# Block-sparse attention with a cosine MLP: tile 2 transposed by DMA, twenty small instructions moved from VectorE to GpSimd, and a new order of the program

## The chip, the cores and the metric

The kernel runs on one core of one Trainium2 chip. The time is that of one execution on the device, in microseconds; a comparison takes the median of several executions. TensorE is called PE below, VectorE DVE, ScalarE ACT, GpSimd POOL, and the queue from which most transfers are issued SP.

## What is computed

An attention over 4 batches of 8 heads, 768 positions and 64 columns, in which most blocks of 32 queries see only their neighbours, the first and last block, and three sampled blocks; then, on its 3072 x 512 result, an MLP whose activation is h cos(h). q, k and v are f32; the two weight matrices lie in DRAM as 64-bit floats.

```python
scores = scale * np.matmul(q, k.transpose(0, 1, 3, 2))
mask = np.abs(blk_i - blk_j) <= window
mask = mask | (blk_i == 0) | (blk_j == 0) | (blk_i == n_blocks - 1) | (blk_j == n_blocks - 1)
for qb in range(n_blocks):
    for kb in sampled_blocks[qb]:
        mask[qb * block:(qb + 1) * block, kb * block:(kb + 1) * block] = True
scores = np.where(mask, scores, -1000000000.0)
scores = scores - np.max(scores, axis=-1, keepdims=True)
attn = np.exp(scores)
attn = attn / (np.sum(attn, axis=-1, keepdims=True) + 1e-09)
...
h = x @ w_in
g = h * np.cos(h)
return (g @ w_out).astype(np.float32)
```

## The kernel before

**Tiles.** The attention runs over 24 tiles of 128 queries, numbered 0 to 23, six to a batch: five sparse ones and one dense (tile 5 is the first dense one). A sparse tile has four units, each with two heads; a dense one has eight. The MLP has 12 steps of two tiles each, and each step computes four column groups up (`m`, L1722) and down again (`d`, L1772). Operands that need more than f16 holds go as a high and a low half, so a matrix product is three products.

**A unit of a sparse tile.** PE makes the scores (L1377, L1386). DVE adds the mask to them and takes the row maxima (`add_max`, L1417), two instructions a unit. One DVE instruction on 128x2 elements (`neg_max`, L1432, operation `nb`) turns the maxima into the bias of the exponentials. ACT takes two exponentials with it (L1438). Then the probabilities must be split in halves and transposed for PE, which is done in one of two ways:

- By PE: three 128x128 f32 transpositions for each head (`p_turn`, operation `PF`, which issues through `turn32` at L1667 or L1669), then the high half by ACT from PSUM (`turned_hi`, L1459) and the low half by DVE (`turned_lo`, L1463; in tiles 0 and 1 by PE and ACT instead). The list `PF` has a 1 for each unit of tiles 0 to 4 that goes so; in the kernel before these are all units of tiles 0, 1 and 2.
- By DMA: ACT writes the high half into a buffer of a ring of three (`p_hi`, L1448), DVE the low half (`p_lo`, L1452), and SP issues one transposing DMA from the ring into one of the three PT buffers (`p_transpose`, L1473, operation `PT`).

Then PE multiplies by the values (`pv`, L1483 for the gathered blocks and L1500 for the rest; L1516 in a dense tile). Each tile's result is normalized (L1539), split (L1541, L1543), and transposed into the MLP's input `xT`, by PE in the tiles whose entry in the list `XF` is 1, by a DMA on SP otherwise (`x_transpose`, L1562).

**Other work beside it.** In the first 180 us the weights are loaded by SP in 32 pieces (`w_load`, L1592, operation `wl`; piece 17's is `wl17`), converted from 64 to 32 bits by DVE (`f64_to_f32`, L1600 to L1604, operation `wc`), scaled and split. A piece lands in a raw buffer, which must have been read by the conversions of an earlier piece before the next load into it is issued: pieces 16 and 17 land where pieces 12 and 13 were. POOL issues the gathers of V blocks (`v_gather`, L1330), four to a sparse tile, and copies K blocks (L1252); these wait for V's buffers, of which there are two.

**The order.** Nothing is ordered at run time but by semaphores: each engine runs its own list in order. These lists are made when the program is built: a planner (`Plan.op` and `Plan.run`) takes each operation with its engine, its predecessors and a place, and issues them by place. The table PLACES gives the place of every operation by its name: `mx2_0_1`, for instance, is `add_max` of tile 2, unit 0, second half. SP runs its transfers in this order as well, and one that has to wait for its source or its destination holds up those behind it.

The bias is made so:

```python
def neg_max(self, n, qc, mx, nb):
    nc, nu = self.nc, qc[:, 5:6]
    if self.seq[n][1] == self.NS:
        nc.vector.tensor_tensor(mx[:, 0:2], mx[:, 0:2], mx[:, 2:4], ALU.max)
    nc.vector.tensor_scalar(nb, mx[:, 0:2], nu, LN_PSCALE, op0=ALU.mult, op1=ALU.add)
```

Of the kernel before, what the change touches and what calls it, by code (L numbers as in the profile page):

```python
# [17 lines left out]
ALU = mybir.AluOpType  # L18
# [7 lines left out]
LN_PSCALE = 14.0 * math.log(2.0)  # L26
# [19 lines left out]
    PF=[1, 1, 1, 1, 1, 1, 1, 1, 1, 1, 1, 1, 0, 0, 0, 0, 0, 0, 0, 0], PC=["ph", "ph"], XF=[1, 1, 1, 0, 0, 0], XC="ph", UF=[1, 1, 1, 1, 0, 0], UC="ph", KF=[1] * 6, KC=["ph"] * 6,  # L46
# [5 lines left out]
    WGP=[0, 1, 1, 1, 1], WCP=[0] * 16, WCE=[0] * 16,  # L52
# [9 lines left out]
idx 0 sx 1 regs2_1 2 regs1_1 3 const_ident 4 ql1 5 qsq1 6 regs0_1 7 kload0_0 8 ksq0_0 9 kload0_1 10 const_pool 11 const_a 12 const_gidx 13 regs1_0 14  # L62
qsp1 15 kload0_2 16 const_samples 17 regs0_0 18 ksq0_1 19 ksq0_2 20 kred0 21 kall0s 22 qsc1c 23 ql0 24 qsc1e 25 regs3_1 26 vload0_0 27 const_b1 28
qsc1s 29 kall0 30 vload0_1 31 qsq0 32 qsp0 33 qsc0c 34 ksc0c 35 qsc0e 36 vload0_2 37 ksc0e 38 qhi1 39 qu0 40 ksc0s 41 vsq0_0 42 qnu0 43 khi0_1_0 44
khi0_1_1 45 qlo1 46 khi0_0_2 47 qsc0s 48 qhi0 49 vsq0_1 50 qu1 51 vsq0_2 52 wl1 53 ql2 54 klo0_1_0 55 klo0_1_1 56 khi0_0_1 57 klo0_0_2 58 wl2 59 qlo0
60 khi0_0_0 61 vred0 62 vall0s 63 klo0_0_1 64 vall0 65 khi0_1_2 66 qsq2 67 vsc0c 68 wc1_0 69 vsc0e 70 regs1_3 71 klo0_1_2 72 vsc0s 73 klo0_0_0 74
vhi0_5 75 ql3 76 vhi0_0 77 qk0_1 78 vhi0_4 79 wl0 80 qk0_0 81 wc1_1 82 vlo0_5 83 const_b 84 const_w 85 vlo0_0 86 vst0_0 87 vlo0_4 88 vhi0_2 89 wgd0 90
qsp2 91 qsc2c 92 wga0 93 qo0_0 94 qk0_2 95 qk0_3 96 qo0_3 97 qo0_2 98 vhi0_1 99 vst0_4 100 vlo0_2 101 vhi0_3 102 vst0_5 103 vlo0_1 104 qsq3 105 qo0_1
106 vst0_2 107 const_c 108 qsc2e 109 mx0_0_0 110 regs4_1 111 wc0_0 112 qsc2s 113 vst0_1 114 vlo0_3 115 mx0_0_1 116 qk1_1 117 const_n 118 mx0_1_0 119
nb0_0 120 wc0_1 121 vst0_3 122 mx0_1_1 123 ex0_0_0 124 wc0_2 125 mx0_2_0 126 ex0_0_1 127 mx0_3_0 128 qsp3 129 mx0_3_1 130 PF0_0_0 131 PF0_0_1 132 qnu1  # L70
133 qhi2 134 wl3 135 nb0_1 136 ex0_1_0 137 ph0_0_0 138 nb0_3 139 ph0_0_1 140 mx0_2_1 141 regs1_2 142 ex0_1_1 143 nb0_2 144 qu2 145 ex0_2_0 146 qk1_0
147 PG0_0_0 148 PG0_0_1 149 wgd1 150 pg0_0_1 151 qlo2 152 ex0_2_1 153 wc1_2 154 wga1 155 qo1_0 156 qo1_1 157 mx1_0_0 158 mx1_0_1 159 qsc3c 160 wl4 161
PF0_1_0 162 wc3_0 163 qsc3e 164 qu3 165 vg0_0 166 PF0_2_1 167 ex0_3_0 168 nb1_0 169 vg1_0 170 ph0_1_0 171 qsc3s 172 PF0_2_0 173 ph0_2_0 174 vg0_2 175
PF0_1_1 176 ph0_1_1 177 PG0_1_0 178 wsq0 179 pg0_1_0 180 wc3_1 181 vi0_0 182 pg0_0_0 183 ex1_0_0 184 vi0_1 185 ph0_2_1 186 mx1_1_0 187 wsq1 188
ex1_0_1 189 qk1_3 190 wl5 191 PG0_2_0 192 PG0_1_1 193 mx1_1_1 194 vg1_1 195 wc3_2 196 wsq3 197 qk1_2 198 pg0_2_0 199 regs2_3 200 vg0_1 201 ex0_3_1 202
PG0_2_1 203 regs3_0 204 wred0 205 wall0s 206 wall0 207 wsc0c 208 pg0_1_1 209 pg0_2_1 210 qnu2 211 nb1_1 212 qo1_3 213 qnu3 214 wc5_0 215 qo1_2 216 ql4
217 qsq4 218 mx1_3_0 219 ex1_1_1 220 qhi3 221 PF0_3_0 222 vi0_3 223 ex1_1_0 224 wc5_1 225 vi0_2 226 wsc0e 227 pv0_0 228 mx1_3_1 229 wsc0s 230 rs0 231
PF0_3_1 232 PF1_0_1 233 po0_0 234 wl7 235 po0_1 236 po0_2 237 ph0_3_0 238 ph0_3_1 239 PG0_3_1 240 whi2 241 wc5_2 242 nb1_3 243 pg0_3_1 244 regs2_0 245
PG0_3_0 246 wl6 247 qsp4 248 pg0_3_0 249 mx1_2_0 250 vi1_1 251 vg1_2 252 rr0 253 pv0_1 254 PF1_0_0 255 wl8 256 wgd2 257 wc7_0 258 whi0 259 ex1_3_0 260
wl9 261 ph1_0_0 262 mx1_2_1 263 pv0_2 264 PF1_1_0 265 wc7_1 266 wga2 267 pv0_3 268 ph1_0_1 269 qk2_0 270 qo2_0 271 mx2_0_0 272 ex1_3_1 273 qsc4c 274  # L80
mx2_0_1 275 PG1_0_0 276 PF1_1_1 277 PG1_0_1 278 vi1_2 279 wsi0 280 qlo3 281 wc7_2 282 ql5 283 qsc4e 284 ph1_1_0 285 pg1_0_0 286 PG1_1_0 287 wlm1 288
nb1_2 289 ph1_1_1 290 pg1_0_1 291 wsq5 292 pg1_1_0 293 nb2_0 294 wl11 295 qk2_1 296 qu4 297 qo2_1 298 PG1_1_1 299 wsq7 300 pg1_1_1 301 vi1_0 302 wlm0
303 pv1_0 304 ex1_2_1 305 mx2_1_0 306 mx2_1_1 307 wred4 308 wc9_0 309 ex1_2_0 310 regs4_3 311 wl10 312 wall4s 313 wlp1 314 po0_3 315 wlp0 316 wall4
317 PF1_3_0 318 ph1_3_0 319 wsc4c 320 PF1_3_1 321 wc9_1 322 wsc4e 323 wlm3 324 pv1_1 325 PF1_2_0 326 ex2_0_0 327 no0 328 PF1_2_1 329 vi1_3 330 qk2_3
331 ph1_3_1 332 regs4_0 333 sce0 334 PG1_3_0 335 vg2_0 336 rs1 337 qo2_3 338 po1_0 339 ex2_0_1 340 wc9_2 341 pg1_3_0 342 mx2_3_0 343 qsq5 344 ph1_2_0
345 PG1_3_1 346 mx2_3_1 347 vi2_2 348 wlp3 349 qsc4s 350 wsc4s 351 rr1 352 ph1_2_1 353 wlm2 354 pg1_3_1 355 wc11_0 356 vi2_1 357 wsi4 358 PG1_2_0 359
PF2_0_0 360 regs3_3 361 nb2_3 362 pg1_2_0 363 wc11_1 364 nb2_1 365 qk2_2 366 whi4 367 qsp5 368 qsc5c 369 qo2_2 370 wl13 371 po1_3 372 po1_1 373 wlp2
374 PG1_2_1 375 PF2_0_1 376 pg1_2_1 377 wlm5 378 wl12 379 wgd3 380 wc11_2 381 qhi4 382 vg2_2 383 wsq9 384 mx2_2_0 385 XF0 386 wl15 387 qsc5e 388 pv1_2
389 mx2_2_1 390 wga3 391 vg2_1 392 ph2_0_0 393 pl2_0_0 394 turn0_0 395 ex2_1_0 396 wlm4 397 qk3_0 398 qo3_0 399 ph2_0_1 400 pl2_0_1 401 nb2_2 402 qu5
403 pv1_3 404 wc13_0 405 mx3_0_0 406 qlo4 407 po1_2 408 wlp5 409 no1 410 xh0 411 whi6 412 ex2_3_1 413 ex2_2_0 414 wsq11 415 ex2_2_1 416 wlm7 417  # L90
ex2_3_0 418 wl14 419 vg3_0 420 wc13_1 421 wred8 422 wc13_2 423 XG0 424 PF2_2_0 425 XF1 426 ph2_2_0 427 wall8s 428 wlm6 429 wall8 430 pl2_2_0 431
ex2_1_1 432 mx3_0_1 433 vi2_3 434 wsc8c 435 PF2_3_1 436 wc15_0 437 PF2_1_0 438 xh1 439 PF2_3_0 440 wsc8e 441 xg0 442 wlp6 443 wc14_0 444 wsq13 445
vi3_2 446 qnu5 447 wlp7 448 qk3_3 449 wc15_1 450 wc14_1 451 qo3_3 452 wlp4 453 ph2_3_0 454 mx3_3_0 455 mx3_3_1 456 ql6 457 nb3_0 458 wc15_2 459
PF2_2_1 460 ph2_3_1 461 wl16 462 rs2 463 wl17 464 pv2_0 465 XG1 466 pl2_3_0 467 qk3_1 468 xg1 469 PF2_1_1 470 ph2_2_1 471 qo3_1 472 qsq6 473 wc14_2
474 wl19 475 ex3_0_0 476 ex3_0_1 477 pl2_3_1 478 nb3_3 479 ex3_3_1 480 vi2_0 481 po2_0 482 wsq15 483 qk3_2 484 pl2_2_1 485 qo3_2 486 ex3_3_0 487 ph3_0
488 mx3_1_0 489 ph2_1_0 490 m0_0_0 491 mx3_1_1 492 mx3_2_0 493 wc17_0 494 qnu4 495 po2_3 496 wsc8s 497 wc17_1 498 m0_0_1 499 vg3_1 500 m0_0_2 501 wgd4
502 ph3_3 503 wc17_2 504 mx3_2_1 505 pv2_2 506 wred12 507 qsc5s 508 wga4 509 pl2_1_0 510 pl3_0 511 wall12s 512 m0_0_3 513 wl18 514 wl25 515 nb3_1 516
whi8 517 wc18_0 518 whi10 519 ph2_1_1 520 vi3_1 521 wl20 522 wc19_0 523 pl2_1_1 524 wsi8 525 ev0_0_0 526 wlm8 527 pv2_1 528 wlm11 529 ev0_0_1 530
wsq17 531 po2_1 532 ka0_0 533 nb3_2 534 pv2_3 535 wall12 536 qk4_0 537 wc18_1 538 qhi5 539 ex3_1_1 540 ex3_2_0 541 rr2 542 wsc12c 543 ex3_2_1 544
ph3_2 545 pl3_3 546 wlp11 547 kb0_0 548 qk4_3 549 wc19_1 550 wc18_2 551 wc19_2 552 pl3_2 553 qo4_0 554 wl21 555 wlm10 556 PT3_0 557 qo4_3 558 wsq18  # L100
559 wsc12e 560 wlp8 561 mx4_0_0 562 mx4_0_1 563 qk4_1 564 vi3_0 565 wsq19 566 mx4_3_0 567 mx4_3_1 568 vg3_2 569 sin0_0 570 nb4_0 571 wred16 572 qo4_1
573 nb4_3 574 PT3_3 575 qk4_2 576 mx4_1_0 577 mx4_1_1 578 wall16s 579 ex3_1_0 580 rs3 581 gm0_0 582 ex4_0_0 583 wlm9 584 po2_2 585 wall16 586 nb4_1
587 wsc12s 588 ph3_1 589 pl3_1 590 rr3 591 wsc16c 592 turn0_1 593 pv3_0 594 wlp10 595 wsc16e 596 qo4_2 597 mx4_2_0 598 wl22 599 wlp9 600 no2 601
ex4_0_1 602 wl23 603 m0_1_0 604 wsi12 605 m0_1_1 606 whi14 607 wsc16s 608 ex4_1_0 609 vi3_3 610 mx4_2_1 611 pv3_3 612 XF2 613 wc21_0 614 nb4_2 615
wc21_1 616 ex4_1_1 617 PT3_1 618 po3_0 619 po3_3 620 qlo5 621 m0_1_2 622 m0_1_3 623 wc21_2 624 gh0_0 625 gl0_0 626 vg5_0 627 ev0_1_0 628 regs4_2 629
# [314 lines left out]
def plan_kernel(env, B, H, S, D, DM, DFF, pr):  # L420

    pl = Plan()
    e = env
    NB = S // BLK
# [17 lines left out]
    def nudge(key, row, col, width):  # L442
        x = row * width + col
        return pr[key][x] if 0 <= x < len(pr[key]) else 0.0
# [1424 lines left out]
```

## Time and profile before

| what | value |
|---|---|
| median of 3 runs | 765.25 us (763.42 to 768.58) |
| the profiled execution's own time | 764.32 us |
| its span from the first to the last instruction | 762.5 us |
| mean granted clock of PE | 0.975 |
| PE busy | 710.7 us, 93% of the span |
| ACT busy | 633.2 us, 83% |
| DVE busy | 612.2 us, 80% |
| POOL busy | 126.4 us, 17% |

So 1.8 us of the execution's time lie around the span. The busy times are sums over the whole span; the stretches differ much, and the rows further down show them by stretch, with the busy time of each engine in it, the granted clock of PE as a share of full speed, and the mean share of the 16 DMA engines that is in use. A line's "idle before" is the time in which its engine stood still just ahead of it, with what ended most of that.

### The profile page before, as it was taken

How to read it: one execution, taken by the hardware profiler on the slowest of the kernel's cores; microseconds unless marked ns; L12 is line 12 of the kernel's file. 1: busy time of each engine (PE TensorE's matmuls, PEld its weight loads, DVE VectorE, ACT ScalarE, POOL GpSimd, SP SyncE). 2: the span in 40 equal slices, each digit the busy share in tenths (PEclk: the TensorE clock that was granted, in tenths of full speed). 3: DMA queues.
4: the chain of work that ended last, by engine and by line, in shares of the span. 5: the costliest groups of instructions: out<-in, count | busy, mean ns of one | idle time of the engine just before them, and what ended most of it. 6: DMA issues, size and time to landing. Idle time of an engine off the chain costs nothing.

```text
span 762.5 us, 24855 instructions
## 1 busy us (share of the span) xinstructions
PE 710.7 (93%) x10286; PEld 484.8 (64%) x10286; DVE 612.2 (80%) x1551; ACT 633.2 (83%) x1210; POOL 126.4 (17%) x164
## 2 busy tenths in 40 slices
PE   3679897999999999999989998999999999999997
PEld 2446563668576568467666676677677677676763
DVE  5979999999999788988968787799878877665361
ACT  4689899999799888999987897998988987866342
POOL 6744402000401201020210302010311020000000
PEclk9589999999999999999999999999999999999999
DMA  7876889688838999999965799897949895446101
GB/s 281 242 234 216 265 198 249 157 216 189 211 90 149 180 191 181 229 208 220 196 112 108 171 185 203 165 206 140 192 79 172 151 174 91 109 102 100 42 1 69
DMA packets 209569, 127.26 MB, mean 167 GB/s; under 512 B 183472, under 2 KB 183600, under 8 KB 209456
## 3 DMA queue, kind: packets, MB, share of 16 engines
q1 hardware_dynamic: 204336, 109.94, 67.2%
q0 software_dynamic: 5120, 15.73, 9.0%
q8 instruction: 80, 1.31, 0.7%
q14 instruction: 33, 0.27, 0.1%
HBM read 68.23 MB, written 12.58 MB: 106 GB/s over the span
## 4 chain that ended last, share of the span: by engine, by line
PE 53%; ACT 17%; DVE 14%; DMA 9%; issue 5%; another core or an unknown queue 1%; SPq 1%; ACTq 0%; DVEq 0%
PE ph L1722 21%; PE ph L1772 20%; ACT P L1438 4%; DMA PT<-ring 3%; PE ph L1377 2%; DMA xT<-n 2%; PE ph L1500 2%; ACT junk L1169 2%; ACT ring L1448 2%; PE ph L1386 2%; PE ph L1516 2%; PE ph L1483 1%; ACT g L1749 1%; DVE P L1417 1%; DMA qs<-in_q_dram 1%
## 5 line engine op out<-in xcount | busy, mean ns | idle before, releaser
L1722 PE MATMUL ph<-xT,w 128*128 128x256 f16 x2304 | 268.2, 274 | 2.9 <-DMA xT<-n 1.9
L1772 PE MATMUL ph<-w,g 128*128 128x512 f16 x1152 | 267.8, 382 | 1.5 <-issue 1.1
L1722 PEld LDWEIGHTS <-w 128*128 128x128 f16 x2304 | 221.7, 98 | 38.7 <-DMA xT<-n 2.9
L1772 PEld LDWEIGHTS <-g 128*128 128x128 f16 x1152 | 108.2, 98 | 122.4 <-issue 8.5
L1330 POOL DMA_INDIRECT V<-scr,gidx x80 | 91.9, 1148 | 464.0 <-PE ph L1483 314.2
L1438 ACT ACTIVATE P<-P,sm 128x352 f32<-128x352 f32 (+1 forms) x224 | 152.5, 683 | 11.5 <-DVE sm L1432 6.9
L1452 DVE TENSOR_TENSOR ring<-P,ring 128x704 f16<-128x704 f32 (+1 forms) x100 | 90.3, 907 | 21.1 <-ACT ring L1448 20.1
L1417 DVE CUSTOM_DVE_ANT_1 P<-ph,bias 128x352 f32<-128x352 f32 x160 | 78.7, 518 | 18.0 <-PE ph L1386 11.9
L1448 ACT CAST ring<-P 128x704 f16<-128x704 f32 (+1 forms) x100 | 78.2, 789 | 7.9 <-DMA PT<-ring 7.0
L1731 ACT ACTIVATE hs<-ph,sm 128x512 f32<-128x512 f32 x96 | 63.2, 679 | 25.3 <-PE ph L1722 18.9
L1754 DVE SCALAR_TENSOR_TENSOR hs<-hs,sm,g 128x1024 f32<-128x1024 f32 x48 | 61.3, 1281 | 20.2 <-ACT g L1749 20.1
L1763 DVE TENSOR_TENSOR g<-hs,g 128x1024 f16<-128x1024 f32 x48 | 58.5, 1220 | 15.9 <-ACT g L1760 14.3
L1749 ACT ACTIVATE g<-g,sm 128x1024 f32<-128x1024 f32 x48 | 54.5, 1146 | 15.5 <-DVE g L1745 15.2
L1745 DVE SCALAR_TENSOR_TENSOR g<-g,hs 128x1024 f32<-128x1024 f32 x48 | 58.6, 1221 | 0.5
L1760 ACT ACTIVATE g<-hs 128x1024 f16<-128x1024 f32 x48 | 50.3, 1048 | 10.0 <-DVE hs L1754 9.9
L1741 DVE TENSOR_SCALAR g<-hs 128x1024 f32<-128x1024 f32 x48 | 33.2, 691 | 16.8 <-ACT hs L1731 16.5
L1377 PE MATMUL ph<-W,U 64*128 64x192 f16 (+1 forms) x960 | 40.2, 225 | 4.3 <-DVE W L1186 2.2
L1438 ACT ACTIVATION_READ_ACCUMULATOR P<-P,sm 128x1 f32 x224 | 43.0, 192 | 0.0
L1500 PEld LDWEIGHTS <-PT 128*128 128x128 f16 x960 | 36.0, 99 | 9.8 <-issue 2.9
L1500 PE MATMUL ph<-V,PT 128*128 128x64 f16 x960 | 40.3, 194 | 1.5 <-issue 0.7
L1377 PEld LDWEIGHTS <-U 64*128 64x128 f16 x960 | 29.3, 98 | 17.8 <-issue 15.1
L1417 DVE CUSTOM_DVE_ANT_1 P<-ph,dbias 128x384 f32<-128x384 f32 x64 | 33.9, 552 | 1.9 <-PE ph L1401 1.6
(163 smaller groups left out, 848.7 us busy)
## 6 DMA issues: line engine op xcount, KB each, us to landing
V<-scr SPq DMA_DIRECT2D x20, 384.0 KB
qs<-in_q_dram SPq DMA_DIRECT2D x24, 256.0 KB
stage<-in_k_dram SPq DMA_DIRECT2D x12, 512.0 KB
w<-in_moe_w_in_dram SPq DMA_DIRECT2D x12, 512.0 KB
w<-in_moe_w_out_dram SPq DMA_DIRECT2D x12, 512.0 KB
V<-scr SPq DMA_DIRECT2D x8, 768.0 KB
scr<-n SPq DMA_DIRECT2D x21, 256.0 KB
out_dram<-ot SPq DMA_DIRECT2D x20, 256.0 KB
```

The source lines that it names most:

```text
L1330: self.nc.gpsimd.indirect_dma_start(V[:96, 2 + j, :], None, self.scr[b][:, :], bass.IndirectOffsetOnAxis(ap=self.gidx[:96, c : c + 1], axi ...
L1377: mm(out, u[r], x, start=(begins and first and not part), stop=(closes and final and part == 1), tile_position=(a * D, 0))
L1417: self.nc.vector.tensor_tensor_reduce(out=self.p_view(n, Pt)[:, a].rearrange("p (n c) -> p n c", c=hf), in0=self.flat32(sp)[:, :w].rearran ...
L1438: self.nc.scalar.activation(Pv[:, a], Pv[:, a], AF.Exp, scale=qc[:, 4:5], bias=nb[:, a : a + 1], accum_out=sums[:, x : x + 1],)
L1448: self.nc.scalar.copy(R[:, :, 0, : self.width(n)], self.p_view(n, Pt))
L1452: self.nc.vector.tensor_tensor(R[:, :, 1, :w], self.p_view(n, Pt), R[:, :, 0, :w], ALU.subtract)
L1500: mm(xp[:, h, :], PT[:, 6 * a + 3 * l + c, :], V[:, c, h, d0:d1], start=(begins and a == 0 and c == 0 and x == 0), stop=(ends and a == 1 a ...
L1722: self.nc.tensor.matmul(ph[:, ff, :], self.W1[p][:, wl, cc, c * P : (c + 1) * P], xT[:, xl * NCC + cc, :], start=(j == 0), stop=(j == len( ...
L1731: self.nc.scalar.activation(hs[:, h * 512 : h * 512 + 512], ph.rearrange("p f t -> p (f t)"), AF.Copy, scale=self.turns[b][:, p : p + 1])
L1749: self.nc.scalar.activation(kt, kt, AF.Sin, scale=-SIN_SCALE, bias=self.halfpi)
L1754: self.nc.vector.scalar_tensor_tensor(hs, hs, c[:, p : p + 1], kt, op0=ALU.mult, op1=ALU.mult)
L1772: self.nc.tensor.matmul(self.flat32(po), g[:, gl, ff, t * P : (t + 1) * P], self.W2[p][:, wl, ff, :], start=(first and ff == half * hf and ...
```

## The change

Four things are changed.

1. The four units of tile 2 go by DMA instead of by PE: the list `PF` has 8 ones instead of 12. For each unit six transpositions on PE, two `turned_hi` and two `turned_lo` go; one `p_hi`, one `p_lo` and one transposing DMA on SP come. Tile 2's x goes by DMA too (`XF`).
2. `neg_max` runs on POOL for sparse tiles with a number under 6 (`NBP=6`), that is for tiles 0 to 4: 20 instructions. The planner's cost for it is .32 us there instead of .13.
3. The table PLACES is another one, so every engine's list is in another order.
4. Two lists that could put conversions of weights on POOL, and held only zeros, are gone. This moves no instruction.

```diff
-    PF=[1, 1, 1, 1, 1, 1, 1, 1, 1, 1, 1, 1, 0, 0, 0, 0, 0, 0, 0, 0], PC=["ph", "ph"], XF=[1, 1, 1, 0, 0, 0], XC="ph", UF=[1, 1, 1, 1, 0, 0], UC="ph", KF=[1] * 6, KC=["ph"] * 6,
+    PF=[1, 1, 1, 1, 1, 1, 1, 1, 0, 0, 0, 0, 0, 0, 0, 0, 0, 0, 0, 0], PC=["ph", "ph"], XF=[1, 1, 0, 0, 0, 0], XC="ph", UF=[1, 1, 1, 1, 0, 0], UC="ph", KF=[1] * 6, KC=["ph"] * 6,
...
-    WGP=[0, 1, 1, 1, 1], WCP=[0] * 16, WCE=[0] * 16,
+    WGP=[0, 1, 1, 1, 1], NBP=6,
...
 PLACES = """
...
-nb0_0 120 wc0_1 121 vst0_3 122 mx0_1_1 123 ex0_0_0 124 wc0_2 125 mx0_2_0 126 ex0_0_1 127 mx0_3_0 128 qsp3 129 mx0_3_1 130 PF0_0_0 131 PF0_0_1 132 qnu1
+432 XG1 433 xg1 434 qk3_3 435 wl17 436 wl16 437 mx3_0_0 438 xg0 439 wc14_2 440 wsq13 441 qo3_3 442 pl2_1 443 qk3_1 444 qk3_2 445 wc15_2 446 qo3_1 447
...
-            op("DVE", 0.13 if sparse else 0.33, pos + at(1) + pr["NB"], lambda mx=mx, nb=nb: e.neg_max(n, qc.t, mx.t, nb.t), r=[mx, u], w=[nb, (mx, 0)], name=f"nb{n}_{j}")
+            pool = n < pr["NBP"] and sparse
+            op("POOL" if pool else "DVE", 0.32 if pool else 0.13 if sparse else 0.33, pos + at(1) + pr["NB"], lambda mx=mx, nb=nb, pool=pool: e.neg_max(n, qc.t, mx.t, nb.t, pool), r=[mx, u], w=[nb, (mx, 0)], name=f"nb{n}_{j}")
...
-    def neg_max(self, n, qc, mx, nb):
+    def neg_max(self, n, qc, mx, nb, pool):
...
-        nc.vector.tensor_scalar(nb, mx[:, 0:2], nu, LN_PSCALE, op0=ALU.mult, op1=ALU.add)
+        (nc.gpsimd if pool else nc.vector).tensor_scalar(nb, mx[:, 0:2], nu, LN_PSCALE, op0=ALU.mult, op1=ALU.add)
```

On SP, in the kernel before, the loads of weight pieces 16 to 21 stand behind one another, with one load of V blocks and that of piece 25 (into g1) between them (w1_3 and w2_3 are raw buffers of the weights, in_moe_w_in and in_moe_w_out the two matrices); the first transposition of P, tile 3's, comes behind them:

```order
L1592 DMA w1_3_67<-in_moe_w_in_dram 128x1024 x2
L1592 DMA w2_3_71<-in_moe_w_in_dram 128x1024
L1324 DMA V0_105<-scr0_124 16x2048
L1592 DMA w2_3_71<-in_moe_w_in_dram 128x1024
L1592 DMA g1_85<-in_moe_w_in_dram 128x1024
L1592 DMA w1_3_67<-in_moe_w_out_dram 128x1024 x2
L1473 DMA_TRANSPOSE PT2_104<-ring0_99 128x12x128
```

In the changed kernel the same loads stand between tile 2's four transpositions:

```order
L1473 DMA_TRANSPOSE PT1_103<-ring0_99 128x12x128
L1592 DMA w1_3_67<-in_moe_w_in_dram 128x1024 x2
L1592 DMA w2_3_71<-in_moe_w_in_dram 128x1024
L1473 DMA_TRANSPOSE PT0_102<-ring1_100 128x12x128
L1592 DMA w2_3_71<-in_moe_w_in_dram 128x1024
L1473 DMA_TRANSPOSE PT2_104<-ring2_101 128x12x128
L1592 DMA w1_3_67<-in_moe_w_out_dram 128x1024
L1473 DMA_TRANSPOSE PT1_103<-ring0_99 128x12x128
L1592 DMA w1_3_67<-in_moe_w_out_dram 128x1024
```

The first transposition is now ahead of pieces 16 and 17, and the others are each ahead of one more piece; SP stands still at one whose ring buffer isn't written yet.

On POOL, in the kernel before, the copies of tile 1's K blocks are followed at once by the first gathers of V blocks (Wg holds the K blocks, V_105 and V_106 are the two V buffers):

```order
L1252 ISA
L1252 COPY Wg_107<-W 128x8x32
L1330 DMA V_106<-scr_124,gidx 96x1024 x2
L1084 TENSOR_LOAD sm
L1330 DMA V_106<-scr_124,gidx 96x1024 x2
L1330 DMA V_105<-scr_124,gidx 96x1024
L1252 ISA
```

In the changed kernel the biases stand between the copies and the gathers:

```order
L1252 ISA
L1252 COPY Wg_107<-W 128x8x32
L1432 TENSOR_SCALAR sm<-sm 128x2 x2
L1330 DMA V_106<-scr_124,gidx 96x1024 x4
L1432 TENSOR_SCALAR sm<-sm 128x2 x3
L1252 ISA
L1252 COPY Wg_107<-W 128x8x32
```

Two biases of tile 0 now stand behind eight copies and ahead of tile 0's gathers, and three of tile 1 behind these gathers.

## Rows read from the trace of the kernel before

**Rows 1.** The page: the span, and busy time of each engine.
```profile
span 762.5 us, 24855 instructions
PE 710.7 (93%) x10286; PEld 484.8 (64%) x10286; DVE 612.2 (80%) x1551; ACT 633.2 (83%) x1210; POOL 126.4 (17%) x164
```
**Rows 2.** Windows: us, busy (instructions) by engine, granted clock, DMA share, GB/s.
```profile
60.00:160.00 100.00, 88.97 (x1445) 58.20 (x1445) 96.35 (x244) 96.52 (x194) 23.49 (x28) 1.00 0.85 217
160.00:260.00 100.00, 99.12 (x1314) 67.05 (x1310) 97.87 (x251) 92.78 (x179) 15.84 (x12) 1.00 0.76 168
260.00:762.50 502.50, 487.00 (x6918) 334.29 (x6916) 373.86 (x898) 403.37 (x745) 51.19 (x48) 0.99 0.75 146
740.00:762.50 22.50, 18.45 (x86) 8.15 (x84) 5.02 (x5) 4.95 (x6) 0.00 (x0) 0.97 0.17 59
```
**Rows 3.** Windows inside the second stretch of rows 2, same columns.
```profile
80.00:100.00 20.00, 16.71 (x365) 11.53 (x361) 19.22 (x50) 18.12 (x39) 7.66 (x11) 1.00 0.88 248
100.00:120.00 20.00, 18.34 (x352) 11.76 (x341) 19.97 (x48) 19.97 (x38) 2.73 (x2) 1.00 0.92 251
120.00:140.00 20.00, 16.03 (x160) 9.19 (x159) 18.51 (x48) 19.58 (x37) 2.86 (x3) 1.00 1.04 203
```
**Rows 4.** PE's transpositions by line L1669 in the window 60 to 115 us.
```profile
60.00:115.00 55.00, 4.65 (x28) 3.15 (x28) 1.00 0.81 222
```
**Rows 5.** Groups by line and shape: the halves of a unit, busy us and mean ns.
```profile
L1459 ACT CAST PT<-ph 128x384 f16<-128x384 f32 x24 | 11.1, 490 | 2.7 <-PE ph L1667 2.4 <-issue 0.3
L1463 DVE TENSOR_TENSOR PT<-ph,PT 128x384 f16<-128x384 f32 x8 | 4.3, 543 | 0.0
L1452 DVE TENSOR_TENSOR ring<-P,ring 128x704 f16<-128x704 f32 (+1 forms) x100 | 90.3, 907 | 21.1 <-ACT ring L1448 20.1
L1448 ACT CAST ring<-P 128x704 f16<-128x704 f32 (+1 forms) x100 | 78.2, 789 | 7.9 <-DMA PT<-ring 7.0
```
**Rows 6.** The line of the bias, L1432: its group, and one window of it.
```profile
L1432 DVE TENSOR_SCALAR sm<-sm 128x2 f32<-128x2 f32 x96 | 21.1, 228 | 1.5 <-DVE sm L1417 0.3
60.00:115.00 55.00, 2.56 (x11) 1.00 0.81 222
```
**Rows 7.** Groups on POOL: small instructions, and gathers.
```profile
L1126 POOL TENSOR_SCALAR bias<-V 128x2 bf16<-128x2 f32 x1 | 0.3, 260 | 0.1
L1163 POOL TENSOR_SCALAR V<-V 128x24 f32<-128x24 f32 x5 | 2.8, 568 | 0.5
L1330 POOL DMA_INDIRECT V<-scr,gidx x80 | 91.9, 1148 | 464.0 <-PE ph L1483 314.2 <-PE ph L1516 67.8 <-PE ph L1214 63.6
```
**Rows 8.** Waits: engine and line, waited for, us in total, times, longest.
```profile
ACT P L1438 <- DVE sm L1432: 6.9, 5, 2.5
```
**Rows 9.** Pieces of the chain that ended last: start us, length us, what.
```profile
78.32 7.97 DMA w<-in_moe_w_in_dram
...
122.70 8.22 DMA xT<-n
...
341.39 10.38 DMA PT<-ring
...
461.20 11.49 DMA PT<-ring
```
**Rows 10.** SP's line L1473: time of one issue (min, median, max ns), and who waited.
```profile
L1473 SPq DMA_TRANSPOSE PT<-ring x100: 1273/1626/4666, 96.5 to 695.9; - x100
```
**Rows 11.** Who waited for the loads of weights, L1592: us, times.
```profile
  DVE stage L1600: 0.2, 1
```

## What was predicted

> **What bounds the kernel now.** I read the page first, then the busy time by stretches, then the chain and the waits in the stretch that the change touches. On the page PE is busy 710.7 of 762.5 us, so it stands still for 51.8 [rows 1]. No change of order can win more than that; only less work for PE can. The stretches say where these 51.8 lie and who holds PE up there. From 160 to 260 us PE is busy 99.12 of 100, and from 260 to the end 487.00 of 502.5 [rows 2]: there PE itself is the bound, and its idle 15.5 us are stalls here and there, 4.05 of them in the last 22.5. From 60 to 160 PE is busy 88.97, while DVE is at 96.35 and ACT at 96.52 [rows 2]. So in these 100 us PE waits 11.0 for results of the other two, and closest from 100 to 120, where ACT and DVE both stand at 19.97 of 20 [rows 3]. What is left, 51.8 - 15.5 - 11.0 - 0.9 = 24.4 us, lies before 60, where the program starts up.
>
> Tile 2's transpositions lie between 60 and 115 us [rows 4], and eleven of the twenty biases too [rows 6]: in the stretch where DVE and ACT are the bound. The reader should keep in mind that an engine is relieved there only as far as the next one lets it: PE has 11.0 us of idle time there already.
>
> **The parts of the change and their cost.** I take edit by edit what it does to each engine, and then what the tightest engine makes of it.
>
> *Tile 2 by DMA, on PE.* The transpositions at L1669 in that stretch are 28, tile 2's 4 x 2 x 3 = 24 and the 4 of its x, and take 4.65 us of PE [rows 4]. They go. Nothing comes to PE for them.
>
> *Tile 2 by DMA, on DVE and ACT.* DVE loses eight `turned_lo`, 4.3 us, and gains four `p_lo` at 0.907, 3.63: net -0.7. ACT loses eight `turned_hi` at 0.490, 3.92, and gains four `p_hi` at 0.789, 3.16: net -0.8 [rows 5]. The halves of tile 2's x cost about the same from SBUF as from PSUM, and I put them at nothing; the cover is that one pair of about 0.6 us each replaces another.
>
> *Tile 2 by DMA, on SP and the DMA engines.* SP gets five transposing DMAs, four for P and one for x. An issue takes 1.3 us at least and 1.6 in the middle [rows 10], so 5 x 1.6 = 8 us of SP's queue. SP has no computation to delay; what it can delay is what stands behind: the loads of pieces 16 to 21 in the order shown. Their latency counts. Piece 17's load was issued at 78.32 and took 7.97 us [rows 9], and at 86.29 DVE's conversion was waiting for it or just came to it: over all loads of weights the waits sum to 0.2 us [rows 11]. So there was no slack and no price. In the new order DVE has 6.9 us of work between the conversion that frees the raw buffer and the one that needs it, where it had 9.2 (sums of the instructions listed between them in the two orders, by their durations in the trace). If the load takes 7.97 again, DVE waits some 1 to 2 us there; if the transpositions between slow it, more. Bounds: 0 if the load is faster, 4 x 3 = 12 if each of the four transpositions takes 3 us off a load. I take 1.5, near the row. A transposition's own way from issue to landing is 10.38 and 11.49 us in the two longest pieces of the chain [rows 9], so PE's products of tile 2 need something ahead of them. In the new order three groups of the MLP's up-product stand there, which stood behind before; I put this wait at nothing, and at 3 us for each of the four units if that cover is too short.
>
> The Trainium skill ("DMA: Bandwidth & Descriptors", section "Latency and other measured facts") gives a transposing DMA an effective 261 GB/s; for one P of 128 x 12 x 128 f16, 393 KB, that would be an estimate of 1.5 us of transfer. The trace agrees for the issue, 1.6 us [rows 10], but not for the landing, which took 10 to 11 us in the rows of the chain; by the page the five would cost 7.5 us of the DMA engines and no wait.
>
> *The biases on POOL.* Twenty instructions leave DVE. One takes 228 ns, and eleven in a window sum to 2.56 us [rows 6]. They overlap their neighbours in part, so DVE gains between 20 x 0.13 = 2.6 (the planner's figure for one, in the diff, in which the overlap is taken off) and 20 x 0.23 = 4.6; I take 3.2. POOL gains 20 instructions. The trace has no f32 one of 128x2; a bf16 one of the same shape takes 260 ns and a 128x24 one 568 [rows 7]. So the bias comes later by 0.03 to 0.34 us each, and 0.6 to 6.8 us in all if ACT waited for every one. ACT's waits for this line are 6.9 us, 5 times [rows 8], all over the program, so it seldom waits for it. Queued behind the biases on POOL are gathers at 1.15 us [rows 7]; a bias that falls behind four gathers is 4.6 us late. By the order shown, the only such place is tile 1's three, behind tile 0's four. I take +1 us in all, and keep 6.8 as the far end.
>
> The Trainium skill ("GPSIMD Engine Reference", section 8, "Key points") says that VectorE is about twice as fast at elementwise work, and that GpSimd shares its SBUF interfaces with VectorE. That speaks against this move. No row here shows the sharing; by the factor of two a bias would take about 0.46 us, an estimate from the 228 ns, and the twenty 4.6 us more, inside the ends just given.
>
> *The order.* It moves nearly everything by a few places; the sums of work on each engine up to the same milestones differ by few us between the two orders, so I can give it no sum of its own. It changes the stalls: the 11.0 us of PE from 60 to 160 and the 15.5 from 260. One of them is the transposition of x of tile 3, issued at 122.70 and landed 8.22 later [rows 9] with the DMA engines at a share of 1.04 [rows 3], for which PE stood still. In the new order tile 4's values take the buffer that is free earlier, so fewer loads precede this transposition. Bounds: -11 (half of what can be refilled, below) to +12.
>
> *The sum.* In the stretch that counts, DVE loses 0.7 + 3.2 = 3.9 us and waits 1.5 more: -2.4. ACT loses 0.8 and may wait 1 more. PE loses 4.65, but with 11.0 of idle time there it can use that only as far as DVE and ACT deliver sooner. Later PE is the bound, and what it didn't have to do counts in full as soon as its waits end. Between ACT's -0.8 and PE's -4.65 I take the middle, -2.7. The profiled execution takes 764.32: 764.32 - 2.7 = 761.6. The median shown is 0.9 above this execution, and I leave that out, since it lies within the three runs.
>
> **The rivals.**
>
> *A: ACT is the bound, and nothing comes of it.* For it: ACT at 19.97 of 20 from 100 to 120 [rows 3], and its net is -0.8, eaten by the bias that comes later. PE's 4.65 us become idle time. Then 764.3 - 0.4 = 763.9. Against it: PE is the bound for the 600 us that follow, and needs fewer instructions from then on.
>
> *B: the new order removes stalls that have nothing to do with tile 2.* PE's idle time from 60 to 160 is 11.0 and from 260 to 740 it is 15.5 - 4.05 = 11.45, together 22.5 [rows 2]. In the rows of the chain single waits for transposed P take 10.38 and 11.49 us from issue to landing [rows 9]. If half of the 22.5 goes, with the parts counted in, 764.3 - 11.2 = 753.1. For it: a list searched for this program can place each of them better. Against it: the old list was made in the same way, and from 160 to 260 nothing is left to win.
>
> *C: the loads of weights are late.* Tile 2's transpositions stand ahead of and between pieces 16 to 21, at a share of the DMA engines of 0.88 to 1.04 [rows 3], and without slack [rows 11]. If each of the four takes 3 us off the loads behind it, DVE stands still for 12 us at L1600 to L1604 in a stretch where it is at 96%, and all that follows comes so much later: 764.3 + 12 - 2.7 = 773.6. It decides from the point where DVE's waits for loads of weights exceed the gain of 2.7 us; below that it is only a part of the forecast. Against it: SP waits for the raw buffer there anyway, so the first issue costs nothing.
>
> *D: the biases are late on POOL.* If each of the twenty holds ACT up by 0.34 us, 764.3 - 2.7 + 6.8 = 768.4. For it: ACT is at 96%. Against it: it waited only 5 times for this line in the whole program [rows 8].
>
> **How the numbers follow.** The forecast, 761.6, has a chance of 0.40; its own range is 757 to 766, from -7 (DVE's and PE's whole gain, and the wait of x) to +1.5. A has 0.10, B 0.27, C 0.17, D 0.06. A measurement of this kernel tells about 1% from no change, 7.7 us: below 757.6 is faster, above 772.9 slower. Then B is faster, 0.27, C slower, 0.17, and the rest, 0.40 + 0.10 + 0.06 = 0.56, within 1%. The range that should hold 8 in 10 goes from just under B's value, 751, to that of C's lower half, 773: outside are the stronger half of B, some 0.1, and half of C, some 0.09.
>
> **What would show it right or wrong.** In the profile after, L1669 has gone from the stretch from 60 to 115, and L1432 stands on POOL with 20 instructions; their mean should be 0.26 to 0.57 us. From 60 to 160 PE's busy time falls by 3 to 4 us, and the program of the first tiles ends about 2 to 3 us sooner; from 160 to 260 PE stays at 99%. DVE's wait for the loads at L1600 to L1604 should be 1 to 2 us; 10 or more would mean C. ACT's waits at L1438 for L1432 (now on POOL) should stay under 8 us; 14 would mean D. PE's idle time after 260 should stay at 15 us; 10 or less would mean B, and then the parts named here were not what decided. The forecast falls if the time lies outside 757 to 766, or if it lies inside because two large effects cancel.

## The result, and the profile after

The changed kernel takes 772.16 us (median of 13 executions, 765.21 to 784.36), the kernel before beside it 766.96 (13, 760.15 to 776.33): ratio 1.0124, with an interval from 1.0085 to 1.0162. A ratio here compares means and leaves out executions over 1.5% above their kernel's fastest, so it can differ from the quotient of the medians beside it. The kernel is slower by about 1%, where 761.6 was forecast, a gain of 0.4%.

The page of the changed kernel, its span and busy times, beside [rows 1]:

```profile
span 769.4 us, 24816 instructions
PE 707.6 (92%) x10258; PEld 482.2 (63%) x10258; DVE 610.0 (79%) x1527; ACT 633.1 (82%) x1206; POOL 142.4 (19%) x184
```

PE has 3.1 us less to do, where 4.65 was forecast, and the span is 6.9 us longer all the same. DVE is busy 2.2 us less and ACT 0.1, where 3.9 and 0.8 were forecast. So PE stands still 10.0 us more: 61.8 instead of 51.8. The windows, with the columns of [rows 2], show where:

```profile
0.00:60.00 60.00, 34.30 (x634) 24.00 (x635) 41.33 (x148) 40.06 (x93) 41.24 (x85) 0.89 0.73 247
60.00:160.00 100.00, 88.01 (x1346) 57.66 (x1344) 95.74 (x231) 94.83 (x187) 34.68 (x40) 0.97 0.98 237
160.00:260.00 100.00, 91.04 (x1212) 62.41 (x1211) 88.41 (x219) 85.28 (x167) 13.16 (x12) 0.97 0.74 164
260.00:769.40 509.40, 494.23 (x7071) 338.14 (x7069) 384.56 (x932) 412.92 (x764) 53.30 (x48) 1.00 0.72 146
```

Idle PE is 25.7 us before 60 (24.4 before the change), 12.0 from 60 to 160 (11.0), 9.0 from 160 to 260 (0.9), and 15.2 behind that (15.5). Eight of the ten lost microseconds lie in the stretch in which, before, PE was busy 99%, DVE 98% and ACT 93% [rows 2], and all three are emptier there now. The last bias on POOL starts at 119.8 us, so that part of the change is over by then.

Not all of the eight need be the program's. These are PE's waits from 160 to 265 us for which the profile shows no cause (it calls them "issue"):

```profile
PE ph L1500 <- issue: 1.9, 3, 1.0
PE ph L1386 <- issue: 1.7, 4, 0.5
...
PE ph L1772 <- issue: 0.7, 1, 0.7
```

They sum to 4.3 us, and such stalls differ from chip to chip (last section). On a chip that has few of them, the changed kernel loses 5.6 us in this stretch instead of 8.1 (6.9 us of idle PE against 1.3 in before, in the last and the second group below).

Two other things can be read. POOL took over the twenty biases; this is line L1432 on POOL, with the time of one (min, median, max ns), what it waited for, and who waited for it:

```profile
L1432 POOL TENSOR_SCALAR sm<-sm x20: 267/268/1891, 32.2 to 119.8; 128x2 f32<-128x2 f32 x20
...
  DVE sm L1417: 24.5, 7
...
  ACT P L1438: 10.9, 4
```

And the waits from 20 to 40 us show what that cost at the start:

```profile
ACT P L1438 <- POOL sm L1432: 9.0, 2, 8.3
...
PE ph L1667 <- ACT P L1438: 6.4, 2, 5.8
```

The first maxima are there at 25 us, but the first bias is done at 32.45 (27.77 before), since POOL is making mask constants until 32.1. ACT waits 8.3 us, and PE for ACT. I took this for the cause at first (theory P below, late biases); the other candidates were the new order (O) and the crowding of transfers by tile 2's transpositions (T).

### The profile page after: what moved, and what is told of

It is laid out like the page before. It is cut to its first block, busy times and chain, and to the rows that moved or that the text cites. A ratio compares the mean times of both kernels' runs of the same rounds, so it can differ in the third digit from the quotient of the medians.

```text
span 769.4 us, 24816 instructions
## 1 busy us (share of the span) xinstructions
PE 707.6 (92%) x10258; PEld 482.2 (63%) x10258; DVE 610.0 (79%) x1527; ACT 633.1 (82%) x1206; POOL 142.4 (19%) x184
## 4 chain that ended last, share of the span: by engine, by line
PE 58%; DVE 17%; ACT 8%; DMA 8%; issue 5%; POOL 1%; another core or an unknown queue 1%; SPq 1%; DVEq 1%; POOLq 0%; ACTq 0%
PE ph L1722 24%; PE ph L1772 21%; DMA PT<-ring 4%; PE ph L1500 3%; DVE P L1417 3%; DVE ring L1452 3%; PE ph L1377 3%; PE ph L1386 2%; DMA xT<-n 2%; ACT P L1438 2%; PE ph L1483 2%; DVE hs L1754 2%; PE ph L1401 2%; ACT junk L1169 1%; PE ph L1516 1%
## 5 line engine op out<-in xcount | busy, mean ns | idle before, releaser
L1772 PE MATMUL ph<-w,g 128*128 128x512 f16 x1152 | 268.6, 383 | 1.4 <-issue 0.7
L1772 PEld LDWEIGHTS <-g 128*128 128x128 f16 x1152 | 109.7, 99 | 121.4 <-issue 7.7
L1330 POOL DMA_INDIRECT V<-scr,gidx x80 | 90.1, 1127 | 463.5 <-PE ph L1483 258.6
L1438 ACT ACTIVATE P<-P,sm 128x352 f32<-128x352 f32 (+1 forms) x224 | 153.1, 685 | 22.9 <-POOL sm L1432 10.9
L1452 DVE TENSOR_TENSOR ring<-P,ring 128x704 f16<-128x704 f32 (+1 forms) x104 | 94.1, 907 | 24.3 <-ACT ring L1448 24.0
L1448 ACT CAST ring<-P 128x704 f16<-128x704 f32 (+1 forms) x104 | 81.5, 791 | 3.4 <-DMA PT<-ring 2.3
L1754 DVE SCALAR_TENSOR_TENSOR hs<-hs,sm,g 128x1024 f32<-128x1024 f32 x48 | 61.2, 1275 | 10.5 <-ACT g L1749 10.5
L1760 ACT ACTIVATE g<-hs 128x1024 f16<-128x1024 f32 x48 | 50.2, 1050 | 15.5 <-DVE hs L1754 15.2
```

Source lines behind the costliest of these rows:

```text
L1330: self.nc.gpsimd.indirect_dma_start(V[:96, 2 + j, :], None, self.scr[b][:, :], bass.IndirectOffsetOnAxis(ap=self.gidx[:96, c : c + 1], axi ...
L1438: self.nc.scalar.activation(Pv[:, a], Pv[:, a], AF.Exp, scale=qc[:, 4:5], bias=nb[:, a : a + 1], accum_out=sums[:, x : x + 1],)
L1448: self.nc.scalar.copy(R[:, :, 0, : self.width(n)], self.p_view(n, Pt))
L1452: self.nc.vector.tensor_tensor(R[:, :, 1, :w], self.p_view(n, Pt), R[:, :, 0, :w], ALU.subtract)
L1754: self.nc.vector.scalar_tensor_tensor(hs, hs, c[:, p : p + 1], kt, op0=ALU.mult, op1=ALU.mult)
L1772: self.nc.tensor.matmul(self.flat32(po), g[:, gl, ff, t * P : (t + 1) * P], self.W2[p][:, wl, ff, :], start=(first and ff == half * hf and ...
```

## The experiments

Kernels of one group ran on the same chip and share its runs of before. The chips differ: before takes 749 to 750 us in three of the groups and 764 to 768 in the other two, so ratios are compared, not times. Prices in us below are worked out from the ratios.

**The parts, in the new and the old order** (before: 749.21 us).

New order, biases on DVE:
```diff
-    WGP=[0, 1, 1, 1, 1], NBP=6,
+    WGP=[0, 1, 1, 1, 1], NBP=0,
```


> The changed kernel with one part undone: the twenty biases of tiles 0 to 4 are back on DVE, all else (tile 2 by DMA, the new order) stays. In the changed kernel's trace the first bias comes at 32.45 us, because POOL is busy with its constants until 32.09, where the kernel before had it at 27.77, and ACT stands still 8.3 us there instead of 2.5. Theory P (late biases): this is the loss, so without it the time falls by 4 to 6 us, to 766 to 768, and PE's idle time from 20 to 60 us from 13.7 to about 10. Theory O (the new order loses 8 us of PE between 160 and 260 us, whatever the biases do): the time stays within 2 us of the changed kernel's 772, or gets 2 to 4 longer, since DVE gets 20 x 0.13 to 20 x 0.23 us of work back in a stretch where it is the bound. Theory T (tile 2's transpositions crowd the transfers): no change beyond 2 us either; it is told apart by the runs on the old order.

Measured: 769.74 us, 1.0203 (1.0138 to 1.0267). There is no sign of the 4 to 6 us that theory P expects, but the changed kernel wasn't on this chip; the last group has the two side by side.

Old order, biases on POOL (PLACES, PF and XF as before, `NBP=6`):

> The kernel before with one part of the change alone: the twenty biases of tiles 0 to 4 on POOL, old order, tile 2 by PE. Theory P (late biases): slower than before by 4 to 6 us, 771 to 773. POOL ends its constants at 25.36 us in the old order and the first maxima are there at 25.67, so if only the late constants of the new order delay the first bias, the price is under 1 us here. Theory O (the order): within 2 us of before, or up to 3 faster, since DVE has 2.6 to 4.6 us less to do. Theory T: no change.

Measured: 763.82 us, 1.0161 (1.0111 to 1.0211). The biases do cost time here, as theory P has it, but 12 us instead of 4 to 6, and by another mechanism. One of PE's waits in this kernel:

```profile
PE ph L1488 <- DMA V<-scr,gidx: 15.1, 6, 4.4
```

L1488 is the product with the gathered values (L1483 before). PE waits 15.1 us, six times, for gathers of V; before, it had no such wait. They are issued by POOL, behind biases that wait for their maxima: in one list in order, a bias that isn't ready holds up a gather that is.

Old order, tile 2 by DMA (`NBP=0`; places derived from those of the removed operations):
```diff
-    PF=[1, 1, 1, 1, 1, 1, 1, 1, 1, 1, 1, 1, 0, 0, 0, 0, 0, 0, 0, 0], PC=["ph", "ph"], XF=[1, 1, 1, 0, 0, 0],
+    PF=[1, 1, 1, 1, 1, 1, 1, 1, 0, 0, 0, 0, 0, 0, 0, 0, 0, 0, 0, 0], PC=["ph", "ph"], XF=[1, 1, 0, 0, 0, 0],
```


> The kernel before with one part of the change alone: tile 2's probabilities and x by DMA, biases on DVE, the old order, in which the high half takes the place of the second of a unit's two transpositions and the DMA the place where the first half was written. Theory T (the transpositions crowd the transfers; DMA share 0.91 and 1.11 at 60 to 100 us instead of 0.69 and 0.88): slower than before by 4 us or more, 771 or longer, with waits of DVE for weights or of PE for the transposed P. Theory O (the order): within 2 us of before, or 1 to 3 faster by PE's 4.65 us less. Theory P: the same as O here.

Measured: 763.09 us, 1.0189 (1.0141 to 1.0237). Who waited for the loads of weights (L1596 here, [rows 11] before), and the window from 80 to 100 us:

```profile
  DVE stage L1604: 6.7, 1
  DVE w L1604: 3.8, 3
...
80.00:100.00 20.00, 8.43 (x169) 6.07 (x168) 10.93 (x32) 11.09 (x23) 7.84 (x11) 0.79 0.96 229
```

This is the predicted rival C in its size, 10.5 us of DVE's waits for weights (0.2 before) where C had 12, but not in its way. C took 3 us off the loads for each of four transpositions; here piece 16's load stands behind one transposition on SP, which stands there until its ring buffer is written, so the load is issued at 88.8 us instead of 77.9. Once issued it lands 5.8 us later, no slower than piece 17's 7.97 before [rows 9]. So for this load it is the place in the queue that hurts, and not the crowding of the transfers that theory T had. PE is busy 8.4 of 20 us.

Old order, both parts:

> The kernel before with both parts of the change, biases of tiles 0 to 4 on POOL and tile 2 by DMA, in the old order. Theory O (the order alone is the loss): 2 to 5 us faster than before, 762 to 765, so some 8 us faster than the changed kernel, which differs from it by the order only. Theories P and T: slower than before by 4 us or more. If the sum of what the two parts do alone comes out here, they don't act on each other.

Measured: 766.21 us, 1.0219 (1.0175 to 1.0263). The two prices, 1.6 and 1.9%, don't add up: the stalls overlap, though PE's gaps ahead of products with gathered values alone sum to 19 us here. Theory O had this kernel 2 to 5 us faster than before, so the new order isn't the whole loss: in the old one the parts cost more. The changed kernel's order has removed both queue stalls: DVE's wait for weights is 1.0 us in its trace, PE's for gathers 0.2.

**The order cut in two** (before: 749.90 us).

The cut joins two tables by rule; `NEW` and `OLD` are the changed kernel's and the earlier one's PLACES:
```python
early = sorted((n for n in NEW if NEW[n] < 790), key=NEW.get)      # or OLD, 893
late = sorted((n for n in OLD if n not in early), key=OLD.get)     # or NEW
PLACES = {n: i for i, n in enumerate(early + late)}
```
Before itself, for its trace:

> The kernel before itself, for its trace on the same chip as the others of this call. If the stalls in which PE waits for nothing that the profile shows (6.8 us in the first trace of before, 10.9 in that of the changed kernel, 0.4 to 1.5 in four other programs on another chip) belong to the program, they are 5 us or more here again; if they belong to the chip or the moment, they are under 2 us in all four runs of this call or over 5 in all four.

Measured: 750.03 us, one execution. PE's stalls without a visible cause (gaps over 60 ns that the profile calls "issue") sum to 0.5 us, and to 0.5 to 2.9 in the four runs of this group, where the first traces of before and of the changed kernel have 6.5 and 9.9: they belong to the chip or the moment.

The changed kernel itself:

> The changed kernel itself, timed against before and traced on the same chip as the runs beside it. All theories: 1 to 2% slower than before. Theory O (the order): PE's idle time between 160 and 260 us is about 8 us more than before's. Theory P (late biases): the first bias is again at 32 us and PE's idle time from 20 to 60 us some 4 us more than before's.

Measured: 763.49 us (median of 12 executions from 751.30 to 766.55), 1.0088 (1.0044 to 1.0132).

New order early, old order late, both parts:

> The changed kernel (tile 2 by DMA, biases on POOL) with the new order only up to about 150 us and the old order from there on. Theory O (the loss lies in the new order between 160 and 260 us): 4 to 8 us faster than the changed kernel beside it, so within 1% of before or better. Theory P (the loss is made in the first 60 us by biases that come late): no more than 2 us from the changed kernel.

Measured: 756.27 us, 1.0105 (1.0057 to 1.0152).

Old order and old parts early, new order late:

> The kernel before (tile 2 by PE, biases on DVE) with the old order up to about 170 us and the new order from there on. Theory O: slower than before by 4 to 8 us, so about as the changed kernel. Theory P: within 2 us of before, since all that is late early in the changed kernel is as before here.

Measured: 757.78 us, 1.0102 (1.0055 to 1.0149). Each half costs 1%, 7.9 and 7.6 us, and the whole change costs no more than one of them, 6.6 us: the prices of the halves don't add up. Neither theory is right alone. Theory O had the first of the two 4 to 8 us faster than the changed kernel, and it is no faster; theory P had the second within 2 us of before. The windows of before, new early and new late, with the changed kernel's from the last group (760.23 us, on another chip where before takes as long) in the second place:

```profile
0.00:60.00 60.00, 37.34 (x650) 27.45 (x651) 44.14 (x164) 40.90 (x97) 35.38 (x77) 0.94 0.79 246
60.00:160.00 100.00, 88.96 (x1394) 57.31 (x1392) 94.19 (x239) 95.10 (x191) 23.91 (x28) 0.98 0.87 220
160.00:300.00 140.00, 138.72 (x2148) 97.99 (x2147) 134.56 (x352) 131.67 (x259) 24.68 (x20) 1.00 0.84 179
```
```profile
0.00:60.00 60.00, 34.19 (x634) 23.59 (x635) 41.58 (x148) 40.29 (x94) 41.77 (x86) 0.77 0.73 248
60.00:160.00 100.00, 87.86 (x1352) 57.63 (x1350) 96.00 (x231) 95.04 (x188) 34.05 (x39) 0.97 0.99 235
160.00:300.00 140.00, 130.80 (x2015) 90.01 (x2014) 124.54 (x337) 122.27 (x244) 17.40 (x16) 0.98 0.86 168
```
```profile
0.00:60.00 60.00, 34.29 (x635) 23.96 (x636) 41.77 (x148) 40.50 (x94) 41.97 (x86) 0.89 0.74 248
60.00:160.00 100.00, 82.78 (x1330) 54.38 (x1330) 94.97 (x231) 95.92 (x190) 33.83 (x39) 0.97 0.99 242
160.00:300.00 140.00, 137.19 (x2161) 96.15 (x2159) 130.38 (x344) 126.58 (x249) 24.52 (x20) 1.00 0.84 171
```
```profile
0.00:60.00 60.00, 37.49 (x651) 27.58 (x652) 44.43 (x164) 41.10 (x97) 35.62 (x77) 0.77 0.78 248
60.00:160.00 100.00, 90.34 (x1437) 58.50 (x1436) 97.44 (x245) 98.15 (x194) 23.20 (x28) 1.00 0.86 227
160.00:300.00 140.00, 133.61 (x2077) 93.19 (x2076) 128.86 (x346) 126.42 (x251) 16.86 (x16) 0.99 0.78 170
```

The third row of each is the one to read. PE's idle time from 160 to 300 us is 1.3 before, 9.2 changed, 2.8 with the old late order back, 6.4 with the new late order behind the old early one. So on a start that is exactly the old one, the late order alone brings 5.1 us of idle PE here. In the first rows PE does some 3 us less by 60 us wherever the early order is new.

The join of two tables has a price of its own, which these two times contain. With the new order early PE waits once just behind the join, until 154.5 us; with the new order late, until 174.7:

```profile
PE ph L1522 <- DMA PT<-ring: 4.1, 1, 4.1
```
```profile
PE ph L1728 <- DVE w L1192: 2.4, 1, 2.4
```

Neither before nor the changed kernel in the last group has the first wait, which is most of the extra idle time from 60 to 160 us (17.2 us against 12.1 in the changed kernel). A wait of the second kind takes 0.7 us in the changed kernel. So the halves by themselves probably cost less than 1% each; how much less wasn't measured.

**Repairs of the start** (before: 767.71 us, on a chip with wide intervals).

The dense tiles' constants behind the first biases, in the changed kernel:
```diff
-... const_c 108 ...
+... const_c 142.5 ...
```


> The changed kernel with one operation moved: the making of the dense tiles' mask bias on POOL (first used by tile 5) stands behind tile 0's four biases and tile 1's K copies instead of ahead of the first bias. In the changed kernel's trace it takes POOL from 24.9 to 32.4 us, and the first bias follows at 32.5. Theory P (late biases in POOL's queue): the first bias comes at about 26 us, ACT's wait for it falls from 8.6 to 2 or 3 us, PE's idle time before 60 us by 4 to 6, and the time by 3 to 6 us from the changed kernel's. Theory O (the order after 160 us is all that counts, what is won before is lost in waits from 60 to 160): the time stays within 2 us of the changed kernel's.

Measured: 785.20 us, 1.0202 (1.0099 to 1.0305). The first bias is done at 26.7, as intended, and nothing is won: the constants now hold up the gathers behind them, the first of which starts at 41.8 us instead of 37.7. By 60 us PE has stood still 32.4 us, where it was 25.7 in the changed kernel's first trace. From 40 to 60 us PE waits

```profile
PE ph L1504 <- ACT PT L1474: 7.7, 1, 7.7
PE ph L1487 <- DMA V<-scr,gidx: 4.7, 1, 4.7
```

The same with the old late order, then that late order with all biases on DVE, and with tile 0's alone on DVE (`pool = 0 < n < pr["NBP"] and sparse`):

> The changed kernel with both suspected causes taken away: the dense bias behind tile 0's biases, and the old order from about 150 us on. If late biases and the late order are the two halves of the loss, the time falls by their sum, to within 2 us of before or up to 4 faster (PE has 4.65 us less to do). If a third cause sits in the part from 60 to 160 us (17.1 us of idle PE there with the new early order and the old late one, 11.1 in before), it stays 4 to 6 us slower than before.

> New order to about 150 us, old order from there, tile 2 by DMA, the biases on DVE. Beside the same with the biases on POOL (756.3 us, 1.0105 of before) it gives the price of POOL alone. Theory P: 3 to 6 us faster than that, within 0.4% of before. Theory O: 2 to 4 us slower than that, because DVE gets its 20 instructions back.

> New order to about 150 us, old order from there, tile 2 by DMA, biases of tiles 1 to 4 on POOL and only tile 0's four back on DVE. Theory P, in its narrow form (only the first biases are late, behind the constants): as the run with all biases on DVE or 1 to 3 us faster. In its wide form (every bias on POOL costs): half way between that run and the one with all on POOL.

Measured: 779.00 us, 1.0200 (1.0130 to 1.0270); 784.50, 1.0171 (1.0049 to 1.0294); 774.43, 1.0154 (1.0090 to 1.0219). The intervals overlap, and the changed kernel wasn't timed on this chip; none is a repair, and none tells P from O.

**Tile 0's biases, and the old order shaken** (before: 763.89 us). The places of the kernel before, moved at random:
```python
{n: v + uniform(-1.5, 1.5) if v >= 900 else v for n, v in OLD.items()}   # late; early: +-3 if v < 900
```


> The changed kernel once more, as the measure for the run f5 on the same chip. All theories: 1 to 2% slower than before; idle PE before 60 us 25 to 27 us, between 160 and 300 us 10 us or more, stalls without a visible cause left out.

> The changed kernel with tile 0's four biases back on DVE, those of tiles 1 to 4 stay on POOL, the new order throughout. Theory P, narrow (only the first biases are late): 2 to 4 us faster than the changed kernel beside it, and ACT's first exponential at 28 us instead of 32.8. Theory that the time before 60 us is made up for by 160 us, where DVE and ACT are full anyway: within 1.5 us of the changed kernel.

Measured: changed kernel 771.06 us, 1.0109 (1.0038 to 1.0181); with tile 0's biases on DVE 773.70, 1.0108 (1.0039 to 1.0177). ACT's first exponential starts at 27.8 instead of 32.8 us, and the ratio doesn't move. The wait at the start, the most striking of the new profile, costs nothing that can be measured here; but with intervals of 0.7% to either side, the 2 to 4 us of theory P's narrow form aren't excluded.

> The kernel before with the places of all operations behind 170 us moved at random by up to 1.5 places, all else as before. If the old order is so finely fitted that any other one loses about 1% (theory F), 4 to 8 us slower than before. If the new late order is worse in itself (theory O), within 2 us of before.

> The kernel before with the places of all operations up to 170 us moved at random by up to 3 places. Theory F: 4 to 8 us slower than before. Otherwise within 2 us of it: then what the early half of the change loses belongs to its parts and to its own order, not to the disturbance.

Measured: shaken late 773.91 us, 1.0144 (1.0099 to 1.0189); shaken early 767.09, 1.0055 (1.0019 to 1.0090). Moving late operations by no more than one and a half places costs 11 us, as much as the whole change; moving the early ones by up to three costs 4. For the late half theory F is borne out, that the old order is so finely fitted that any other loses: the new late order needn't be worse than any other that wasn't searched for. Windows of the kernel shaken late, and of before on the chip of the second group:

```profile
470.00:490.00 20.00, 15.53 (x293) 11.91 (x293) 9.69 (x28) 15.27 (x35) 0.00 (x0) 0.91 1.01 176
570.00:590.00 20.00, 16.70 (x201) 10.44 (x199) 13.80 (x34) 14.30 (x25) 4.40 (x4) 0.83 0.62 142
```
```profile
470.00:490.00 20.00, 19.66 (x262) 12.40 (x262) 18.30 (x51) 19.30 (x36) 2.64 (x2) 1.00 0.91 184
570.00:590.00 20.00, 20.00 (x304) 12.15 (x302) 14.79 (x44) 16.62 (x30) 3.70 (x4) 1.00 1.04 191
```

At 474 us PE waits 4.5 for one transposed P; from 570 to 590 its waits are stalls without a visible cause, 3.3 us, of which this chip has more. The two traces are of different chips and the first is of the slowest of six executions, so the rows show where time goes and not how much the shaking costs; the ratio does that, as before ran on the same chip.

**The biases as a whole, side by side** (before: 749.86 us).

> The changed kernel, the measure for the run beside it. Slower than before by 1 to 2%.

> The changed kernel with all twenty biases back on DVE, beside the changed kernel on one chip. If the move to POOL gains what DVE is relieved of (2.6 to 4.6 us), this is 2 to 5 us slower than the changed kernel. If the biases wait in POOL's queue as long as DVE gains, within 2 us of it. If theory P holds, 3 to 6 us faster.

Measured: changed kernel 760.84 us, 1.0154 (1.0109 to 1.0199); with the biases back on DVE 766.95, 1.0242 (1.0204 to 1.0280). The intervals don't overlap: in the order that was made for it, the move to POOL gains 6.6 us, so theory P in its wide form, that the biases on POOL are the loss, falls. In the old order the same move cost 12. No version tried beats the kernel before.

## Why the prediction was wrong

*PE's work, right in kind.* No instruction of L1669 is left from 60 to 115 us; PE is busy 3.1 us less over the span, where 4.65 was the sum of the removed transpositions. But from 60 to 160 us its busy time fell by 1.0 us, where 3 to 4 was the sign set for being right.

*DVE and the loads of weights, about right.* A wait of 1.5 us was put, at piece 17; there is none there, and 1.0 us at a later piece. The time, 772.16, lies close to rival C's 773.6, but that is chance: C's sign was 10 us of DVE's waits for loads. Such waits are real in the old order, 10.5 us, and the new order keeps clear of them. The cover for tile 2's transposed P holds too: PE's gaps ahead of transposed P sum to 0.1 us from 60 to 160.

*The biases, a sign that hangs on the order.* DVE's gain was put at 3.2 us and the cost at 1; side by side the move gains 6.6 us in the new order and costs 12 in the old one, where biases stand ahead of gathers. The durations were put at 0.26 to 0.57 us: the median is 0.268, the mean 0.58 (11.6 us in 20). I said that by the order shown tile 1's three were the only late ones, and overlooked that POOL's list starts with constants: tile 0's first is 4.7 us later. ACT's waits for POOL, 10.9 us in the whole program, lie between the 8 and the 14 that I set as marks for and against rival D. Yet taking tile 0's wait out gained nothing that can be measured (1.0108 beside 1.0109).

*The order, the step that failed.* I wrote that it "moves nearly everything by a few places" and gave it "no sum of its own"; the bounds reached from -11 to +12, and the forecast took nothing. That is the step that the runs contradict: the late order alone, on the old start and without either part, costs 7.6 us (1.0102, from 1.0055 to 1.0149), as much as the whole change on that chip, though no part of the change touches that stretch. Some of it is the join (2.4 us of PE's wait), but shaking the old late places without any join costs 1.4%. And the argument for B, that a list searched for this program can place stalls better, had a reverse that I gave no chance: from 160 to 260 us the old list left 0.9 us of idle PE [rows 2], so another list could hardly win there and could lose much. That from 160 to 260 PE stays at 99% was assumed; it fell to 91%, and to 93% on a chip with few stalls of no visible cause. What was full by the fit of the order was read as full by the nature of the work.

*The size, not fully shared out.* The early half costs 7.9 us with both parts, the new early order and a join in it; which of these it is, stays open, and so does why the two halves together cost no more than one. The new order with tile 2 back on PE wasn't tried.

## What to carry to other kernels

Where a searched order keeps an engine at 99%, that fullness is a property of this order: price a new order from the idle time that the old one doesn't have, as a loss, before counting what the new instructions save. Cut the order in two and run both halves to see which stretch pays, but look at the join first: here PE waited 4.1 and 2.4 us just behind it. And an instruction that waits should not be put on a queue that issues transfers for others (biases ahead of gathers, transpositions ahead of loads) without moving these ahead of it.

## What the runs showed of the hardware that I had not expected

*POOL beside DVE.* A bias of 128x2 took 267 or 268 ns in 11 of 20 cases and up to 1891. Two in a row on POOL, and DVE at the same time, in the changed kernel:

```profile
108.17 3.06 POOL L1432 TENSOR_SCALAR sm<-sm 128x2 f32<-128x2 f32 x2 [2.08 <-DVE sm L1417]
```
```profile
107.90 1.22 DVE L1604 SCALAR_TENSOR_TENSOR stage<-w,stage 128x1024 int32<-128x1024 int32 x1
...
109.15 1.23 DVE L1186 SCALAR_TENSOR_TENSOR w<-stage,sm,w 128x1024 f16<-128x1024 f32 x1
110.30 0.88 DVE L1452 TENSOR_TENSOR ring<-P,ring 128x704 f16<-128x704 f32 x1
```

The two biases take 3.06 us, and their end at 111.2 is that of DVE's run of instructions with two inputs from SBUF (L1604, L1186, L1452). It isn't a single case: six of the twenty ran for more than 0.1 us beside such an instruction, these six took 477 to 1891 ns, and each ended 0.05 to 0.14 us behind the end of one. The other fourteen took 267 to 665 ns. The Trainium skill ("GPSIMD Engine Reference", section 8, "Key points") names such a contention for DVE instructions with two SBUF inputs; this trace agrees. The sampled mask's constants fit it at the start: sixteen small instructions run on POOL from 11.8 to 24.1 us, while DVE is busy 12.29 of these 12.39 us; before, they ran from 9.0 to 15.0, while DVE was busy 3.43 of 6.03. The last of them takes 1.65 us, 0.90 before:

```profile
22.49 1.65 POOL L1148 TENSOR_SCALAR bias<-V 128x30 bf16<-128x30 f32 x1
```
```profile
14.13 0.90 POOL L1148 TENSOR_SCALAR bias<-V 128x30 bf16<-128x30 f32 x1
```

*The clock of PE behind a stall.* In the changed kernel's first trace PE stands still again and again from 248 us on, with no cause that the trace shows, and the granted clock then stands at its lower level, 1.2 GHz:

```profile
248.00:254.00 6.00, 2.37 (x61) 1.41 (x62) 1.93 (x8) 3.09 (x8) 3.65 (x4) 0.76 0.80 188
254.00:258.00 4.00, 4.00 (x15) 1.51 (x13) 2.13 (x7) 1.88 (x5) 0.00 (x0) 0.50 0.70 146
```

Six products of L1772 take 2.75 us from 253.98 on, where six take 1.46 us at the full clock (at 253.59 in the trace of before). So a stall costs more than its own length: from 160 to 300 us the granted clock is 0.96 in the changed kernel's first trace and 0.99 in that of before.

*Stalls without a cause, by chip.* Summed over a trace (PE's gaps over 60 ns that the profile calls "issue") they are 0 to 2.9 us, in any program, on the chips where before takes 749 to 750 us, and 5.6 to 14.3 where it takes 764 to 768. What makes them stays open.
